# The sign of the converted weights carried through ScalarE's exponent (Prelu) instead of a VectorE operation, with the order list written anew

## The chip, the cores and the metric

The kernel runs on one core of one Trainium2 chip. The metric is the device time of one execution in microseconds (us); lower is better.

## The reference

Eight batches of attention between 512 tokens and 32 state rows in each of eight heads, both ways, give 8 x 544 rows of 512 numbers. A feed-forward layer with a rational activation follows. The weights `w_in` and `w_out`, and the coefficients, come as float64 in the kernel's inputs; the kernel turns the weights into float32 itself.

```python
scores = scale * x @ state.T ; a = softmax(scores) ; xread = a @ state      # per batch, head
scores2 = scale * state @ x.T ; a2 = softmax(scores2) ; sread = a2 @ x
rows = concat([xread, sread])                                               # 8 * 544 rows of 512
h = rows @ w_in                                                             # 512 -> 2048
P = a[0] + a[1]*h + a[2]*h**2 + a[3]*h**3
Q = 1 + abs(b[0])*abs(h) + abs(b[1])*h**2
out = (P / (Q + 1e-6)) @ w_out                                              # 2048 -> 512
```

## The kernel before

**The work.** The product of the state with `w_in` is made first for each batch and each slice of the 2048 columns ("extra", `X`, L612: 32 calls of 32 matrix products), stored in DRAM (`XS`) and read back later (`lm`). A step n (72 of them: eight column slices for each of eight batches, then eight for the state rows) then does: `F` (front, L693, twelve TensorE products of 128x512 into the PSUM tile `h`), on ScalarE `FC` (L705), `FB` (L712), `qa` (L732), `ln` (L798) and `ex` (L808), on VectorE `mu`, `po`, `qd`, `g1`, `g2`, `g3` (L716, L720, L726, L737, L743, L749), on GpSimd `gl` (L756), and on TensorE `mh` and `ml` (L766), which multiply the results `gh` and `gl` with `w_out`: four products for each of four row tiles from `gh`, two from `gl`. So `gh` (`g1`, L737) is what lets TensorE go on with a step.

**The weights.** Each float64 arrives as two 32-bit words in a tile `raw` (`lr`, DMA, 16 of 512 KB for each weight). There are 16 groups of two raw tiles: eight for `w_in`, eight for `w_out`. Per group, ScalarE runs `cp` twice (L300): it reads the upper word as a float32 and scales it by 2^-112, so that the exponent field loses its bias and the value can be shifted; the sign stays in the top bit. VectorE runs `jr` twice (L309, the low three mantissa bits out of the lower word), then `jl` (L320: the upper word shifted left by three, or-ed with these bits) and `js` (L331: the sign bit of the upper word or-ed in; its output is the tile `win_sb` for `w_in` and `cv_r` for `w_out`). After that, `X` reads `win_sb`, and `sp` (L342, L343) splits `cv_r` for `w_out` into two float32r tiles.

**What sets the order.** Each engine works through its own instructions in the order of a list of words in `ORDER` (L23), written out by hand or by a planner: a word such as `jl:3` calls the function in the table `ops` (L824) with these numbers, and so puts its instructions at the end of its engine's queue. Nothing else orders the work; an instruction then waits only for what it reads and for the buffer that it writes. All DMAs go through SyncE's queue in the list's order. The group conversions are spread over the first part of the list, between the first steps; all 16 groups are done before `g1` of step 8.

**The table of functions.** ScalarE's tables of functions are loaded once, at the start (L226), with a set that has Exp and Ln in it.

Of the kernel before, what the change touches and what calls it, by code (L numbers as in the profile page):

```python
# [13 lines left out]
AF = mybir.ActivationFunctionType  # L14
# [178 lines left out]
def attention_rational_ffn(  # L193
# [7 lines left out]
    nc = tc.nc  # L201
# [737 lines left out]
```

## Time and profile before

| | |
|---|---|
| median of 3 runs | 705.17 us (704.26 to 705.89) |
| the profiled execution | 705.25 us, of which 703.5 us are the span from the first to the last instruction |
| TensorE (PE) | 669.0 us busy (95%) |
| VectorE (DVE) | 655.5 us busy (93%) |
| ScalarE (ACT) | 523.5 us busy (74%) |
| GpSimd (POOL) | 300.4 us busy (43%) |
| mean granted TensorE clock | 0.978 of full speed |

The span is what the trace shows; 1.75 us of the execution's time lie around it. Busy time is the union of an engine's instructions. For TensorE it counts a product from its start to its modelled end, and neighbouring products overlap, so it is read best in stretches: whether the engine had a gap there, and what ended the gap. The span has two parts that are read apart: one in which the weights are converted beside the first steps (up to about 149 us), and the rest.

### The profile page before, as it was taken

How to read it: one execution, taken by the hardware profiler on the slowest of the kernel's cores; microseconds unless marked ns; L12 is line 12 of the kernel's file. 1: busy time of each engine (PE TensorE's matmuls, PEld its weight loads, DVE VectorE, ACT ScalarE, POOL GpSimd, SP SyncE). 2: the span in 40 equal slices, each digit the busy share in tenths (PEclk: the TensorE clock that was granted, in tenths of full speed). 3: DMA queues.
4: the chain of work that ended last, by engine and by line, in shares of the span. 5: the costliest groups of instructions: out<-in, count | busy, mean ns of one | idle time of the engine just before them, and what ended most of it. 6: DMA issues, size and time to landing. Idle time of an engine off the chain costs nothing.

```text
span 703.5 us, 11586 instructions
## 1 busy us (share of the span) xinstructions
PE 669.0 (95%) x4602; PEld 527.4 (75%) x4602; DVE 655.5 (93%) x605; ACT 523.5 (74%) x641; POOL 300.4 (43%) x172
## 2 busy tenths in 40 slices
PE   5788898999999999999999999999999899999997
PEld 3545565677778788878877878787878788888896
DVE  5898998999999999999999999999899989989996
ACT  4888797787766778787668687867777668667673
POOL 0033233563455445534454354435444443555542
PEclk8879999999999999999999999999999999999999
DMA  7989777513221331331311402210414001400311
GB/s 278 348 289 367 254 276 260 187 65 105 76 66 69 105 121 46 136 105 60 120 31 49 146 22 100 75 55 20 150 48 163 5 25 62 133 1 1 121 61 30
DMA packets 29434, 81.49 MB, mean 116 GB/s; under 512 B 3268, under 2 KB 3396, under 8 KB 29380
## 3 DMA queue, kind: packets, MB, share of 16 engines
q1 hardware_dynamic: 29380, 80.75, 33.2%
q8 instruction: 36, 0.59, 0.3%
q14 instruction: 18, 0.15, 0.1%
HBM read 52.95 MB, written 27.79 MB: 115 GB/s over the span
## 4 chain that ended last, share of the span: by engine, by line
PE 59%; DVE 22%; issue 4%; ACT 4%; POOL 1%; DMA 1%; SPq 0%; POOLq 0%; DVEq 0%; ACTq 0%
PE h L693 18%; DVE gh L737 4%; DVE A L743 3%; DVE A L726 3%; DVE C L716 3%; DVE C L749 3%; DVE C L720 3%; PE o__6016 L766 2%; PE o__2487 L766 2%; PE o__2431 L766 2%; PE o__5464 L766 2%; PE o__5498 L766 2%; PE o__6001 L766 2%; PE o__5476 L766 2%; PE o__2436 L766 2%
## 5 line engine op out<-in xcount | busy, mean ns | idle before, releaser
L756 POOL TENSOR_TENSOR gl<-C,L 128x1024 fp32r<-128x1024 f32 (+1 forms) x71 | 172.7, 2433 | 302.5 <-DVE C L749 223.6
L693 PE MATMUL h<-aT,m 128*128 128x512 f32 x768 | 190.0, 392 | 3.8 <-ACT xo L624 2.5
L693 PEld LDWEIGHTS h<-aT,m 128*128 128x128 f32 x768 | 142.7, 188 | 36.9 <-ACT xo L624 4.2
L705 ACT ACTIVATE C<-h,cst 128x1024 f32<-128x1024 f32 (+1 forms) x72 | 83.2, 1155 | 42.7 <-PE h L693 34.5
L712 ACT ACTIVATE A<-h,cst 128x1024 f32<-128x1024 f32 (+1 forms) x72 | 76.5, 1066 | 45.1 <-PE h L693 39.4
L743 DVE SCALAR_TENSOR_TENSOR A<-A,gh 128x1024 f32<-128x1024 f32 (+1 forms) x72 | 94.8, 1317 | 1.7
L732 ACT ACTIVATE A<-A 128x1024 f32<-128x1024 f32 (+1 forms) x72 | 72.7, 1011 | 30.2 <-DVE A L726 30.1
L737 DVE SCALAR_TENSOR_TENSOR gh<-C,cst,L 128x1024 fp32r<-128x1024 f32 (+1 forms) x72 | 91.8, 1275 | 3.5 <-ACT L L808 1.0
L749 DVE SCALAR_TENSOR_TENSOR C<-C,cst,A 128x1024 f32<-128x1024 f32 (+1 forms) x72 | 91.3, 1269 | 2.0
L726 DVE SCALAR_TENSOR_TENSOR A<-A,b0a,h 128x1024 f32<-128x1024 f32 (+1 forms) x72 | 87.0, 1211 | 6.3 <-ACT A L712 4.4
L716 DVE TENSOR_TENSOR C<-C,h 128x1024 f32<-128x1024 f32 (+1 forms) x72 | 83.1, 1155 | 8.1 <-ACT C L705 7.3
L720 DVE SCALAR_TENSOR_TENSOR C<-C,cst,h 128x1024 f32<-128x1024 f32 (+1 forms) x72 | 87.8, 1220 | 2.1
L653 POOL TENSOR_TENSOR m<-m_sb,m 128x512 fp32r<-128x512 f32 x56 | 76.7, 1379 | 28.6 <-ACT m L652 19.9
L798 ACT ACTIVATE L<-A 128x1024 f32<-128x1024 f32 (+1 forms) x72 | 73.0, 1014 | 3.2 <-POOL gl L756 0.3
L808 ACT ACTIVATE L<-L 128x1024 f32<-128x1024 f32 (+1 forms) x72 | 73.0, 1014 | 1.5
L612 PE MATMUL ps_x<-win_sb,st 64*32 64x256 f32 x1024 | 39.6, 437 | 9.9 <-DVE C L720 3.7
L343 POOL TENSOR_TENSOR wo<-cv_r,wo 128x512 fp32r<-128x512 f32 x16 | 21.9, 1382 | 56.5 <-ACT wo L342 56.3
L612 PEld LDWEIGHTS ps_x<-win_sb,st 64*32 64x32 f32 x1024 | 18.6, 119 | 26.6 <-issue 14.2
L624 ACT COPY xo<-ps_x 128x1024 f32<-128x1024 f32 (+1 forms) x32 | 29.0, 912 | 8.7 <-PE ps_x L612 4.6
L652 ACT CAST m<-m_sb 128x512 fp32r<-128x512 f32 x56 | 33.8, 613 | 0.0
L300 ACT ACTIVATE cv_y<-raw 128x512 f32<-128x512 f32 x32 | 21.4, 682 | 6.5 <-DMA raw<-in_w_in_dram 5.3
L693 PEld LDWEIGHTS h<-sh,m 128*128 128x128 f32 x192 | 24.1, 191 | 0.6
(267 smaller groups left out, 1163.9 us busy)
## 6 DMA issues: line engine op xcount, KB each, us to landing
m_sb<-m_dram SPq DMA_DIRECT2D x56, 256.0 KB, 3.3
m_dram<-xo SPq DMA_DIRECT2D x24, 512.0 KB, 3.4
out_dram<-o_sb SPq DMA_DIRECT2D x34, 256.0 KB, 4.3
raw<-in_w_in_dram SPq DMA_DIRECT2D x16, 512.0 KB, 6.1
xT_sb<-in_xT_dram SPq DMA_DIRECT2D x16, 512.0 KB, 5.1
raw<-in_w_out_dram SPq DMA_DIRECT2D x16, 512.0 KB, 6.0
x_sb<-in_x_dram SPq DMA_DIRECT2D x16, 512.0 KB, 5.2
w_in_dram<-win_sb SPq DMA_DIRECT2D x8, 512.0 KB, 5.0
```

The lines of the kernel that those rows point to most:

```text
L653: nc.gpsimd.tensor_tensor(m[:, 1], t, m[:, 0].bitcast(F32), op=ALU.subtract)
L693: nc.tensor.matmul(h[:, ci * W : (ci + 1) * W], l, r, start=(q == 0), stop=(q == len(seq) - 1),)
L705: nc.scalar.activation(e["C"], e["h"], AF.Identity, scale=cst[:, 3:4], bias=cst[:, 2:3])
L712: nc.scalar.activation(e["A"], e["h"], AF.Abs, scale=cst[:, 5:6])
L716: nc.vector.tensor_tensor(e["C"], e["C"], e["h"], op=ALU.mult)
L720: nc.vector.scalar_tensor_tensor(e["C"], e["C"], cst[:, 1:2], e["h"], op0=ALU.add, op1=ALU.mult)
L726: nc.vector.scalar_tensor_tensor(e["A"], e["A"], b0a, e["h"], op0=ALU.add, op1=ALU.mult)
L737: nc.vector.scalar_tensor_tensor(e["gh"], e["C"], cst[:, 0:1], e["L"], op0=ALU.add, op1=ALU.mult)
L743: nc.vector.scalar_tensor_tensor(e["A"], e["A"], 1.0 + 1e-6, e["gh"].bitcast(F32), op0=ALU.add, op1=ALU.mult)
L749: nc.vector.scalar_tensor_tensor(e["C"], e["C"], cst[:, 0:1], e["A"], op0=ALU.add, op1=ALU.subtract)
L756: eng.tensor_tensor(e["gl"], e["C"], e["L"], op=ALU.mult)
L766: nc.tensor.matmul(O[t], e[l][:, j * W + t * P : j * W + (t + 1) * P], wo[:, k, 2 * u + j, :], start=(place == FIRST[n // U, t] and i + j ...
```

## The change

`cp` uses the function Prelu with alpha = 2^32 in place of Copy. A positive value is only scaled by 2^-112, as before. A negative one is multiplied by 2^32 as well, which adds 32 to its exponent field; since that field is small after the scaling, this sets a bit of it that is free otherwise. The shift by three in `jl` moves that bit into the place of the sign. So `js` has nothing left to do: it goes, 16 calls in all, and `jl` writes `win_sb` itself for `w_in`. `ORDER` is a new list: it has the same calls apart from the 16 `js`, in another order throughout.

```diff
@@ conv_parts
         nc.scalar.activation(
             CV[k][0][:, j].bitcast(F32),
             RAW[i][:, :, 1].bitcast(F32),
-            AF.Copy,
+            AF.Prelu,
             scale=2.0**-112,
+            alpha=2.0**32,
         )
@@ join_low
     def join_low(k):
-        y, r = CV[k]
-        nc.vector.scalar_tensor_tensor(
-            r, y, 3, r, op0=ALU.logical_shift_left, op1=ALU.bitwise_or
-        )
-
-    def join_sign(k):
         what, u = groups[k]
         y, r = [t.rearrange("p j f -> p (j f)") for t in CV[k]]
         w = r
         if what == "in":
             win_t[u] = ld.tile([P, NP, CW], F32, name="win_sb", tag="win", bufs=3)
             w = win_t[u].rearrange("p c f -> p (c f)").bitcast(I32)
         nc.vector.scalar_tensor_tensor(
-            w, y, -(2**31), r, op0=ALU.bitwise_and, op1=ALU.bitwise_or
+            w, y, 3, r, op0=ALU.logical_shift_left, op1=ALU.bitwise_or
         )
@@ ops
         "jl": join_low,
-        "js": join_sign,
@@ ORDER
...
```

Line numbers of the changed kernel are a few lower: `cp` is L299, `jl` L325, `X` L606, `F` L687, `mh` and `ml` L760, `po` L714, `mu` L710, `qd` L720, `g1` L731, `fo` L635.

**VectorE, where the third and fourth group are joined, just ahead of the first steps' `qd`.** Before:

```order
L320 SCALAR_TENSOR_TENSOR cv_r<-cv_y,cv_r 128x1024
L331 SCALAR_TENSOR_TENSOR win_sb<-cv_y,cv_r 128x1024
L641 TENSOR_TENSOR m<-ps_x,m 128x512
L309 TENSOR_SCALAR cv_r<-raw 128x512 x2
L320 SCALAR_TENSOR_TENSOR cv_r<-cv_y,cv_r 128x1024
L331 SCALAR_TENSOR_TENSOR cv_r<-cv_y,cv_r 128x1024
L726 SCALAR_TENSOR_TENSOR A<-A,b0a,h 128x1024
```

Now:

```order
L635 TENSOR_TENSOR m<-ps_x,m 128x512
L309 TENSOR_SCALAR cv_r<-raw 128x512 x2
L325 SCALAR_TENSOR_TENSOR win_sb<-cv_y,cv_r 128x1024
L309 TENSOR_SCALAR cv_r<-raw 128x512 x2
L720 SCALAR_TENSOR_TENSOR A<-A,b0a,h 128x1024
L325 SCALAR_TENSOR_TENSOR cv_r<-cv_y,cv_r 128x1024
```

Two operations per group are one now, and the first `qd` stands ahead of the fourth group's join.

**ScalarE, from the start of its queue** (`cv_y` is what `cp` writes; the rows with `e` are Exp). Before:

```order
L226 ACT_TABLE_LOAD
L300 ACTIVATE cv_y<-raw 128x512 x2
L251 COPY cst<-ps_c__122 128x6
L420 COPY sT<-ps_sc__126 128x512
L420 COPY sT<-ps_sc__125 128x512
L300 ACTIVATE cv_y<-raw 128x512
L453 ACTIVATE e_190,r_191<-sT,cm 128x512
L300 ACTIVATE cv_y<-raw 128x512
L496 ACTIVATE e_170<-e_170 128x512
```

Now:

```order
L225 ACT_TABLE_LOAD
L299 ACTIVATE cv_y<-raw 128x512 x2
L250 COPY cst<-ps_c__131 128x6
L414 COPY sT<-ps_sc__112 128x512
L414 COPY sT<-ps_sc__113 128x512
L299 ACTIVATE cv_y<-raw 128x512
L631 CAST m<-ps_x 128x512
L618 COPY xo<-ps_x 128x512
L447 ACTIVATE e_178,r_179<-sT,cm 128x512 x2
```

The conversions keep their places among the Exp calls, and the load at the start is the only table load among the 590 rows of either queue.

**TensorE, after the front products of step 15** (`h` rows are `F`, `gh` and `gl` rows are `mh` and `ml`). The last row is, in both, the first product that reads step 15's `gh`. Before, step 15's `F` ends 70 products ahead of it, five rows above this piece:

```order
L766 MATMUL o__1800<-wo,gl 128x512 x2
L766 MATMUL o__1823<-wo,gl 128x512 x4
L693 MATMUL h<-aT,m 128x512 x6
L766 MATMUL o__1828<-wo,gl 128x512 x2
L766 MATMUL o__1828<-wo,gh 128x512 x4
L693 MATMUL h<-aT,m 128x512 x6
L766 MATMUL o__1828<-wo,gl 128x512 x2
L766 MATMUL o__1800<-wo,gh 128x512 x4
L693 MATMUL h<-aT,m 128x512 x6
L766 MATMUL o__1837<-wo,gh 128x512 x4
L693 MATMUL h<-aT,m 128x512 x6
L766 MATMUL o__1837<-wo,gh 128x512 x4
```

Now it ends 54 products ahead, two rows above this piece:

```order
L760 MATMUL o__1804<-wo,gl 128x512 x4
L687 MATMUL h<-aT,m 128x512 x12
L760 MATMUL o__1819<-wo,gl 128x512 x2
L760 MATMUL o__1852<-wo,gl 128x512 x2
L760 MATMUL o__1814<-wo,gl 128x512 x2
L760 MATMUL o__1804<-wo,gl 128x512 x2
L760 MATMUL o__1814<-wo,gh 128x512 x4
L760 MATMUL o__1852<-wo,gh 128x512 x4
L687 MATMUL h<-aT,m 128x512 x12
L760 MATMUL o__1814<-wo,gh 128x512 x4
L760 MATMUL o__1819<-wo,gl 128x512 x2
L760 MATMUL o__1814<-wo,gh 128x512 x4
```

So 16 products fewer stand between step 15's `F` and the first reader of its `gh`.

## Rows read from the trace of the kernel before

**Rows 1.** The busy time of the engines in four stretches of the span: the start up to the first `g1` (43.54 us), the same from VectorE's first uninterrupted work on (11.01 us), from there to the eighth `g1` (148.75 us), and the rest up to TensorE's last product. Columns: the stretch, its length; busy us (number of instructions) of PE, PE's weight loads, DVE, ACT, POOL; granted TensorE clock as a share of full speed, DMA share, GB/s.

```profile
0.00:43.54 43.54, 30.16 (x409) 18.96 (x413) 33.84 (x49) 30.17 (x47) 3.23 (x8) 0.78 0.81 305
11.01:43.54 32.53, 24.28 (x359) 15.02 (x363) 30.36 (x44) 26.75 (x42) 2.53 (x2) 0.76 0.80 299
43.54:148.75 105.21, 94.34 (x1154) 62.43 (x1147) 97.38 (x102) 86.55 (x115) 40.28 (x24) 0.96 0.74 262
148.75:699.00 550.25, 544.45 (x3052) 446.04 (x3050) 524.27 (x457) 406.21 (x479) 256.90 (x140) 1.00 0.22 73
```

**Rows 2.** Groups of instructions: line, engine, operation, output and inputs, shapes, number | busy us, mean ns of one | idle time of the engine before them, and what ended it. First the conversion's own lines, then other ScalarE operations of the same shape or of the table.

```profile
L331 DVE SCALAR_TENSOR_TENSOR win_sb<-cv_y,cv_r 128x1024 int32<-128x1024 int32 x8 | 10.8, 1345 | 0.3
L331 DVE SCALAR_TENSOR_TENSOR cv_r<-cv_y,cv_r 128x1024 int32<-128x1024 int32 x8 | 9.8, 1221 | 0.2
L320 DVE SCALAR_TENSOR_TENSOR cv_r<-cv_y,cv_r 128x1024 int32<-128x1024 int32 x16 | 20.5, 1280 | 2.6 <-ACT cv_y L300 2.0
L300 ACT ACTIVATE cv_y<-raw 128x512 f32<-128x512 f32 x32 | 21.4, 682 | 6.5 <-DMA raw<-in_w_in_dram 5.3 <-DMA raw<-in_w_out_dram 1.3
L342 ACT CAST wo<-cv_r 128x512 fp32r<-128x512 f32 x16 | 9.6, 618 | 0.5 <-DVE cv_r L331 0.5
L453 ACT ACTIVATE e<-sT,cm 128x512 f32<-128x512 f32 x16 | 11.5, 720 | 2.8 <-DVE cm L434 2.7
L226 ACT ACT_TABLE_LOAD x1 | 1.3, 1283 | 0.7 <-PEq L919 0.7
```

**Rows 3.** VectorE's instructions in order of time: start us, duration us, line, operation, output and inputs, shapes, number [idle time before it and what ended it]. The five `js` ahead of the first `g1`, what follows the first of them, that first `g1`, the last `js`, and the eighth `g1`.

```profile
7.66 1.22 DVE L331 SCALAR_TENSOR_TENSOR win_sb<-cv_y,cv_r 128x1024 int32<-128x1024 int32 x1
11.01 0.69 DVE L424 TENSOR_REDUCE cm<-sT 128x1 f32<-128x512 f32 x1 [2.12 <-ACT sT L420]
19.57 1.23 DVE L331 SCALAR_TENSOR_TENSOR win_sb<-cv_y,cv_r 128x1024 int32<-128x1024 int32 x1
27.15 1.22 DVE L331 SCALAR_TENSOR_TENSOR win_sb<-cv_y,cv_r 128x1024 int32<-128x1024 int32 x1
31.08 1.22 DVE L331 SCALAR_TENSOR_TENSOR cv_r<-cv_y,cv_r 128x1024 int32<-128x1024 int32 x1
41.80 1.23 DVE L331 SCALAR_TENSOR_TENSOR win_sb<-cv_y,cv_r 128x1024 int32<-128x1024 int32 x1
43.54 1.28 DVE L737 SCALAR_TENSOR_TENSOR gh<-C,cst,L 128x1024 fp32r<-128x1024 f32 x1
...
140.29 1.23 DVE L331 SCALAR_TENSOR_TENSOR cv_r<-cv_y,cv_r 128x1024 int32<-128x1024 int32 x1
148.75 1.28 DVE L737 SCALAR_TENSOR_TENSOR gh<-C,cst,L 128x1024 fp32r<-128x1024 f32 x1
```

**Rows 4.** TensorE's waits between 11 and 149 us, longest first: engine, the waiting tile and line <- whom it waited for: us in total, times, longest us.

```profile
PE ps_x L612 <- DVE C L720: 3.7, 1, 3.7
PE ps_x L612 <- ACT xo L624: 3.7, 3, 2.2
PE h L693 <- ACT xo L624: 2.5, 3, 1.6
PE ps_x L612 <- DVE e L472: 2.3, 1, 2.3
PE ps_e L440 <- DVE m L641: 2.1, 1, 2.1
PE h L693 <- DVE C L720: 1.2, 1, 1.2
PE o__652 L766 <- ACT sr L557: 1.0, 1, 1.0
```

**Rows 5.** One piece of the chain of work that ended last, in the second part of the span: start us, us, engine, tile, line, number of instructions.

```profile
156.38 2.72 PE h L693 x12
```

**Rows 6.** Step 15 in order of time (columns as in rows 3), on three engines: its last front products (the first six of a run of 18), its `FB` on ScalarE, its `g1` on VectorE, and the first TensorE products that read `gh` of step 15.

```profile
212.16 4.24 PE L693 MATMUL h<-aT,m 128*128 128x512 f32 x18
```

```profile
213.72 1.12 ACT L712 ACTIVATE A<-h,cst 128x1024 f32<-128x1024 f32 x1 [2.66 <-PE h L693]
223.63 1.28 DVE L737 SCALAR_TENSOR_TENSOR gh<-C,cst,L 128x1024 fp32r<-128x1024 f32 x1
229.65 1.07 PE L766 MATMUL o__1837<-wo,gh 128*128 128x512 f32 x4
```

327 rows, old and new, of the table ORDER are left out of this document.

## The prediction

> **What bounds the kernel now.** I read the busy time by stretches first, because the page's totals mix two parts that have different limits. After the eighth `g1` TensorE has work in 544.45 of 550.25 us, at a granted clock of 1.00, and twelve of its 128x512 products take 2.72 us on the chain that ended last, 0.227 us each [rows 1, 5]. VectorE has work in 524.27 of these 550.25 us, 95%. So from 149 us on TensorE sets the pace, and what could be won there is its 5.8 us without work. Ahead of that it is another picture. Between 43.54 and 148.75 us VectorE is the engine with the largest share, 97.38 of 105.21 us (93%), with TensorE at 94.34 (90%), ScalarE at 86.55 (82%) and the DMA engines at 0.74 [rows 1]. Between 11.01 and 43.54 us VectorE works 30.36 of 32.53 us, again 93%, while TensorE has gaps and a granted clock of 0.76, a mean between its two levels, 1.2 and 2.4 GHz [rows 1]. TensorE's waits say the same: those with a releaser of their own add up to 16.5 us between 11 and 149 us, 9.3 of them for VectorE (3.7 + 2.3 + 2.1 + 1.2) and 7.2 for ScalarE [rows 4]. The reader is to see in them that the early part is held by VectorE and that TensorE is close behind. Since everything after 149 us is a queue of TensorE work, time that TensorE gains early is kept to the end.
>
> **The change, part by part.** *The 16 sign operations.* They are 10.8 + 9.8 = 20.6 us of VectorE [rows 2], and all lie between 7.66 and 141.52 us [rows 3], in the part that VectorE holds. What of it shortens the span is limited by the engine that comes next, so I take the two stretches apart.
>
> *Up to the first `g1`.* Five of the 16 lie here [rows 3], 6.1 us. Behind the first VectorE sits idle for 2.12 us until ScalarE's copy of the scores is there [rows 3], so its 1.22 us stay hidden. The other four, 4.9 us, lie in the stretch in which VectorE has only 2.2 us of gaps [rows 1]. The bounds are 0 (the raw tiles arrive no sooner: the DMA share is 0.80 here, and ScalarE and TensorE are at 82% and 75% [rows 1]) and 4.9. I take 3.5, nearer the upper end, as no other engine is within ten points of VectorE's share.
>
> *From the first to the eighth `g1`.* The other eleven lie here, 20.6 - 6.1 = 14.5 us. Without them VectorE's work in the stretch is 97.4 - 14.5 = 82.9 us, less than TensorE's 94.34 and ScalarE's 86.55 [rows 1]. So TensorE takes over. If it never waited, the stretch would be 94.3 us, 10.9 shorter; the lower bound is 0, if the waits for ScalarE and the DMAs simply take the places of those for VectorE. In the later part TensorE reaches 99% with VectorE at 95%; here it would run beside ScalarE at 86.55 of about 97 us, 89%. I take 97% for TensorE, 94.34 / 0.97 = 97.3 us, 7.9 us shorter. TensorE could also get shorter itself, as the clock of the stretch is 0.96 [rows 1]: at 1.00 that is up to 4% of 94.3, 3.8 us; I keep it for the upper end. The waits of TensorE for VectorE, 9.3 us, are a check from another side: 3.5 + 7.9 = 11.4 is of their size, a little over.
>
> *Prelu for Copy on ScalarE*, 32 calls of 0.682 us [rows 2]. The trace has no Prelu. The nearest rows of the shape 128x512 are the plain cast of L342, 0.618, and the Exp of L453 with its own bias and sum, 0.720 [rows 2]: that is 32 x -0.064 = -2.0 to 32 x 0.038 = +1.2 us of ScalarE. I take 0: it is the same instruction with the same operands except one constant. ScalarE at 82 to 89% hides either; if it were the bound, all of it would show.
>
> *`jl` into `win_sb`.* Eight of the 16 `jl` now write the tile that `js` wrote. `js` into `win_sb` took 1.345 us on average, with one of 2.19 among them, and into `cv_r` 1.221 [rows 2]; `jl` takes 1.280 now. At most 8 x 0.12 = 1.0 us on VectorE, hidden once TensorE is the bound: 0. The DMAs are the same in number and size.
>
> *The list.* It has the same calls apart from `js`, and no engine's work grows. What it can change is TensorE's waits. After 149 us there are 5.8 us to win; what can be lost is a rival below. I take 0.
>
> **The sum.** 3.5 + 7.9 = 11.4 us less, all at the side of TensorE. The profiled execution took 705.25 us (span 703.5), next to the median of 705.17, so the forecast is 705.25 - 11.4 = 693.8 us.
>
> **The rivals.** *All of it comes back.* If TensorE's clock rises with fewer gaps and the waits for ScalarE go too, the 20.6 us come off whole: 705.25 - 20.6 = 684.7. For it: the granted clock of 0.76 ahead of 43.54 us, which shows what fuller work could give back [rows 1]. Against it: TensorE, ScalarE and the DMAs would all have to be above 90% at once. 10%.
>
> *The other engines hold the early part anyway.* Each of them has 74 to 90% there [rows 1], and the 7.2 us of waits for ScalarE can grow by what those for VectorE shrink. In full this is no change, 704 to 706 us; 7%. Half of the forecast, 698 to 703, is likelier; 13%. For it: six of TensorE's waits are for an `xo` copy on ScalarE, and they add up to 6.2 us [rows 4]; against it: ScalarE is nowhere as full as VectorE.
>
> *Slower: the new list starves TensorE in the later part.* The place is the stretch between a step's `F` and its first `mh`. For step 15 the list before has 70 products in it, 70 x 0.227 = 15.9 us, and the new one 54, 12.3 us. In the trace step 15's `F` ends at about 213.6 us (six products into the run that starts at 212.16), its `gh` is done at 224.9, 11.3 us later, and is read at 229.65: 4.7 us to spare [rows 6]. With 3.6 us less cover, 1.1 us are left. The point from which it decides is a chain from `F` to `gh` that is over 1.1 us longer than this one. If each of the 56 steps from 8 to 63 lost 0.3 us so, that would be 17 us, against 11.4 won: 705.25 + 17 - 11.4 = 711. Against it: on average over these steps I count 19.6 us of cover before and 18.8 now, with the smallest the same, 12.3; and the new list queues `qd`, `qa`, `ln`, `ex` and `g1` of step 15 without another step's between them, where the old one put step 16's and 17's between. 6%.
>
> *Slower: Prelu is not in the loaded table.* Each change between Prelu and Exp or Ln would then need a load. By the list I count 27 such changes; the load at the start took 1.283 us [rows 2], so 34.6 us more of ScalarE. Its work up to the eighth `g1` would be 30.17 + 86.55 + 34.6 = 151.3 us [rows 1], above the 148.75 that the part takes; at 93%, VectorE's share now, it would be 162.7 us, and the time 705.25 + 14 = 719. Against it: the changed ScalarE queue has one table load among its 590 rows, as before. 2%. The Trainium skill, "ScalarE: Activation LUTs", in "Table sets: the hidden batching unit", speaks against mixing functions: functions are loaded in named sets, and for the set with Exp and Ln it names these two and leaves the rest open; it counts about 2.7 us for every switch. By that figure the 27 changes would be an estimated 72 us of ScalarE and the time some 40 us longer again. No run here shows yet which functions the set holds.
>
> **How the numbers follow.** The likeliest case, TensorE taking over from VectorE in the early part, has 62%: 693.8, by its bounds 689 to 698. With the whole gain 10%, half of it 13%, none 7%, slower 6 + 2%. The range of 8 in 10 goes from 686 (a part of the whole gain) to 702 (most of the half gain): it leaves out the 7% of no change, the 8% of slower and about 5% more at its ends. A measurement of this kernel tells some 0.2%, 1.4 us, from no change. Faster by more than that, below 703.8: 62 + 10 + 13 = 85%. Within it: 7%. Slower: 8%.
>
> **What would show it.** Right: one join per group on VectorE and some 20 us less work there; the eighth `g1` at about 137 us in place of 148.75; TensorE's waits for VectorE ahead of it below 3 us, its clock there above 0.96; the stretch after it still about 550 us with TensorE without gaps; `cp` at 0.65 to 0.72 us. It is wrong if the eighth `g1` comes as early as forecast and the time doesn't (the list then loses it later), if `cp` takes over 0.75 us, if a second table load appears, or if the eighth `g1` stays where it is with ScalarE or a raw tile ahead of VectorE.

## The result: 689.75 us, 2.2% less, and the profile after

The changed kernel takes 689.75 us (median, 689.24 to 690.54), the kernel before beside it 705.53. The ratio is 0.978, with a 95% interval of 0.9761 to 0.9798. The forecast was 693.8 us, in a range of 686 to 702. In the profiled executions the span goes from 703.5 to 688.7 us.

The busy times by stretches, cut at the same places as [rows 1]: up to the first `g1`, from there to the eighth, and the rest up to TensorE's last product (columns as in [rows 1]).

```profile
0.00:43.81 43.81, 30.56 (x450) 19.06 (x450) 28.43 (x47) 30.29 (x48) 3.22 (x8) 0.84 0.83 306
43.81:140.94 97.13, 89.86 (x1099) 60.51 (x1100) 84.64 (x88) 85.16 (x115) 42.41 (x24) 0.98 0.80 283
140.94:684.30 543.36, 541.47 (x3054) 445.73 (x3052) 507.02 (x457) 408.07 (x480) 253.07 (x140) 1.00 0.22 74
```

Each stretch less the same one of before:

| stretch | forecast | measured |
|---|---|---|
| up to the first `g1` | -3.5 | 43.81 - 43.54 = +0.3 |
| first to eighth `g1` | -7.9 | 97.13 - 105.21 = -8.1 |
| eighth `g1` to TensorE's last product | 0 | 543.36 - 550.25 = -6.9 |
| together | -11.4 | -14.7 |

So one term is right in size, one came to nothing, and the largest gap is in a stretch in which I expected no change. In that last stretch VectorE runs as many instructions as before, 457, in 507.02 us in place of 524.27.

The conversion's groups, for [rows 2], columns as there:

```profile
L299 ACT ACTIVATE cv_y<-raw 128x512 f32<-128x512 f32 x32 | 21.9, 695 | 11.1 <-DMA raw<-in_w_in_dram 8.7 <-DMA raw<-in_w_out_dram 2.4
L325 DVE SCALAR_TENSOR_TENSOR win_sb<-cv_y,cv_r 128x1024 int32<-128x1024 int32 x8 | 10.9, 1358 | 0.5 <-ACT cst L250 0.3
L325 DVE SCALAR_TENSOR_TENSOR cv_r<-cv_y,cv_r 128x1024 int32<-128x1024 int32 x8 | 9.7, 1215 | 0.4
```

One join per group is left, as long as before. The Prelu takes 0.695 us in place of 0.682, and now waits 11.1 us for raw tiles where it waited 6.5.

TensorE's longest waits between 11 and 141 us, for [rows 4]:

```profile
PE ps_x L606 <- ACT xo L618: 6.1, 4, 2.7
PE ps_x L606 <- DVE C L714: 4.6, 1, 4.6
PE ps_x L606 <- DVE r L479: 1.0, 1, 1.0
```

The longest pieces of the chain of waits between 43 and 141 us (start us, us, what):

```profile
46.72 7.47 DMA raw<-in_w_in_dram
...
70.00 6.02 DMA m_dram<-xo
...
79.90 3.96 DMA m_dram<-xo
...
87.13 7.10 DMA raw<-in_w_in_dram
...
103.11 4.91 DMA m_dram<-xo
```

`xo` is the copy of the extra product on ScalarE (L618), and `m_dram<-xo` its store. The reader is to see that up to 109 us the chain now runs through raw loads, stores and the `xo` copies between them: they are 39 of its 65 us there. From 109 to 141 us TensorE's products are 26 of 32. VectorE has 5 us of the whole.

TensorE's waits behind 149 us, first of the kernel before, then of the changed one:

```profile
PE o__4881 L766 <- POOL gl L756: 1.8, 1, 1.8
PE ps_sr L566 <- ACT sr L557: 1.5, 1, 1.5
PE o__3121 L766 <- POOL gl L756: 0.9, 1, 0.9
PE ps_e L440 <- ACT L L808: 0.8, 1, 0.8
```

```profile
PE o__4923 L760 <- POOL gl L750: 1.0, 1, 1.0
PE o__2418 L760 <- POOL gl L750: 0.5, 1, 0.5
PE o__1819 L760 <- POOL gl L750: 0.4, 1, 0.4
```

### The profile page after: what moved, and what is told of

Same layout as the page of the kernel before. It is cut to its first block, busy times and chain, and to the rows that moved or that the text cites. A ratio compares the mean times of both kernels' runs of the same rounds, so it can differ in the third digit from the quotient of the medians.

```text
span 688.7 us, 11564 instructions
## 1 busy us (share of the span) xinstructions
PE 661.9 (96%) x4602; PEld 525.3 (76%) x4602; DVE 620.1 (90%) x589; ACT 524.1 (76%) x641; POOL 298.7 (43%) x172
## 4 chain that ended last, share of the span: by engine, by line
PE 77%; DVE 7%; DMA 6%; ACT 5%; issue 2%; POOL 1%; SPq 0%; POOLq 0%; ACTq 0%; DVEq 0%
PE h L687 25%; DMA m_dram<-xo 3%; DMA raw<-in_w_in_dram 2%; ACT xo L618 2%; PE o__3063 L760 2%; PE ps_x L606 2%; PE o__5992 L760 2%; PE o__3659 L760 2%; PE o__4266 L760 2%; PE o__3652 L760 2%; PE o__3604 L760 2%; PE o__5977 L760 2%; PE o__5430 L760 2%; PE o__3107 L760 2%; PE o__4244 L760 2%
## 5 line engine op out<-in xcount | busy, mean ns | idle before, releaser
L750 POOL TENSOR_TENSOR gl<-C,L 128x1024 fp32r<-128x1024 f32 (+1 forms) x71 | 168.9, 2379 | 271.1 <-DVE C L743 170.0
L687 PE MATMUL h<-aT,m 128*128 128x512 f32 x768 | 188.6, 392 | 0.8 <-ACT xo L618 0.8
L687 PEld LDWEIGHTS h<-aT,m 128*128 128x128 f32 x768 | 143.1, 188 | 33.1 <-ACT xo L618 2.9
L731 DVE SCALAR_TENSOR_TENSOR gh<-C,cst,L 128x1024 fp32r<-128x1024 f32 (+1 forms) x72 | 95.6, 1328 | 13.1 <-ACT L L802 9.5
L720 DVE SCALAR_TENSOR_TENSOR A<-A,b0a,h 128x1024 f32<-128x1024 f32 (+1 forms) x72 | 87.4, 1214 | 14.2 <-ACT A L706 10.4
L647 POOL TENSOR_TENSOR m<-m_sb,m 128x512 fp32r<-128x512 f32 x56 | 75.0, 1348 | 46.1 <-ACT m L646 22.0
L743 DVE SCALAR_TENSOR_TENSOR C<-C,cst,A 128x1024 f32<-128x1024 f32 (+1 forms) x72 | 91.0, 1263 | 2.1
L714 DVE SCALAR_TENSOR_TENSOR C<-C,cst,h 128x1024 f32<-128x1024 f32 (+1 forms) x72 | 87.7, 1219 | 1.9
L737 DVE SCALAR_TENSOR_TENSOR A<-A,gh 128x1024 f32<-128x1024 f32 (+1 forms) x72 | 87.5, 1216 | 1.7
L710 DVE TENSOR_TENSOR C<-C,h 128x1024 f32<-128x1024 f32 (+1 forms) x72 | 83.0, 1154 | 5.3 <-ACT C L699 2.7
L606 PE MATMUL ps_x<-win_sb,st 64*32 64x256 f32 x1024 | 39.6, 432 | 12.3 <-ACT xo L618 6.1
L337 POOL TENSOR_TENSOR wo<-cv_r,wo 128x512 fp32r<-128x512 f32 x16 | 23.3, 1476 | 59.8 <-ACT wo L336 59.6
L606 PEld LDWEIGHTS ps_x<-win_sb,st 64*32 64x32 f32 x1024 | 18.5, 116 | 28.1 <-issue 10.8
L618 ACT COPY xo<-ps_x 128x1024 f32<-128x1024 f32 (+1 forms) x32 | 28.8, 908 | 5.3 <-DMA m_dram<-xo 4.1
L299 ACT ACTIVATE cv_y<-raw 128x512 f32<-128x512 f32 x32 | 21.9, 695 | 11.1 <-DMA raw<-in_w_in_dram 8.7
L687 PEld LDWEIGHTS h<-sh,m 128*128 128x128 f32 x192 | 24.1, 191 | 0.6
```

What stands on the lines that cost most here:

```text
L647: nc.gpsimd.tensor_tensor(m[:, 1], t, m[:, 0].bitcast(F32), op=ALU.subtract)
L687: nc.tensor.matmul(h[:, ci * W : (ci + 1) * W], l, r, start=(q == 0), stop=(q == len(seq) - 1),)
L710: nc.vector.tensor_tensor(e["C"], e["C"], e["h"], op=ALU.mult)
L714: nc.vector.scalar_tensor_tensor(e["C"], e["C"], cst[:, 1:2], e["h"], op0=ALU.add, op1=ALU.mult)
L720: nc.vector.scalar_tensor_tensor(e["A"], e["A"], b0a, e["h"], op0=ALU.add, op1=ALU.mult)
L731: nc.vector.scalar_tensor_tensor(e["gh"], e["C"], cst[:, 0:1], e["L"], op0=ALU.add, op1=ALU.mult)
```

## The experiments

The change has two parts that can be had apart: the removal of the 16 `js` (with Prelu), and the new list. The list again has an early half, with the conversions, and a later one. The place at which both halves can be joined is the ninth `g1`, when TensorE has about the same 3010 products left in either list. The table has every run that takes these apart; times are the median of the runs, and in us of the profiled execution the eighth and ninth `g1` and what follows the ninth up to TensorE's last product.

| kernel | early list | `js` | later list | median | 8th `g1` | 9th `g1` | rest |
|---|---|---|---|---|---|---|---|
| before | old | yes | old | 705.53 | 148.75 | 158.81 | 540.19 |
| Prelu alone | old | yes | old | 705.65 | 149.32 | 159.40 | 540.09 |
| old list without `js` | old | no | old | 701.25 | 143.73 | 153.60 | 539.95 |
| old, then new | old | no | new | 695.38 | 147.69 | 157.56 | 533.64 |
| new list with `js` | new | yes | new | 705.82 | 155.42 | 165.48 | 533.07 |
| new, then old | new | no | old | 698.28 | 141.22 | 151.32 | 540.55 |
| after | new | no | new | 689.75 | 140.94 | 151.04 | 533.26 |

### The removal alone, in the old list

```diff
 kernel before, ORDER without its 16 words js:0 to js:15
-            AF.Copy,
+            AF.Prelu,
             scale=2.0**-112,
+            alpha=2.0**32,
...
-            w, y, -(2**31), r, op0=ALU.bitwise_and, op1=ALU.bitwise_or
+            w, y, 3, r, op0=ALU.logical_shift_left, op1=ALU.bitwise_or
```

> The change's arithmetic in the old list: Prelu in the conversions, the 16 sign operations gone, every other call in its old place. Theory, the sign operations' 20.6 us of VectorE are what the early part was held by: most of the gain comes without a new list, the eighth g1 at 137 to 142 us (148.75 before) and a time of 691 to 697 us. Rival, the new list carries the gain because the old one was laid out around the sign operations: VectorE only gets gaps where they stood, the eighth g1 at 146 us or later, and 701 to 705 us.

Measured: 701.25 us (699.77 to 702.63), ratio 0.9935 (0.9912 to 0.9959). The removal alone gives 4 us: the theory fell. The rival held in the time, but not in the eighth `g1`, which is at 143.73 us where it had 146 or later. VectorE's longest waits between 11 and 144 us show where room went:

```profile
DVE cv_r L311 <- DMA raw<-in_w_in_dram: 4.0, 2, 2.4
DVE cm L420 <- ACT sT L416: 3.7, 1, 3.7
DVE A L722 <- ACT C L701: 3.3, 2, 2.0
DVE m L637 <- ACT m L633: 2.7, 3, 1.1
```

In the kernel before, the longest of these was 2.1 us, and all with a name came to 9.9 us; here they come to 22.8. VectorE was freed and then waited in its old order for raw tiles and ScalarE. These waits alone don't tell the two lists apart, as they come to 18.2 us in the changed kernel. The chain of waits does: between the first and the eighth `g1` VectorE still has some 31 of its 100 us here, and 5 of 97 in the changed kernel.

### The list alone, with the sign operations put back

```diff
 changed kernel, a word js:k behind each jl:k
-            AF.Prelu,
+            AF.Copy,
             scale=2.0**-112,
-            alpha=2.0**32,
...
+        nc.vector.scalar_tensor_tensor(
+            r, y, 3, r, op0=ALU.logical_shift_left, op1=ALU.bitwise_or
+        )
+    def join_sign(k):
...
-            w, y, 3, r, op0=ALU.logical_shift_left, op1=ALU.bitwise_or
+            w, y, -(2**31), r, op0=ALU.bitwise_and, op1=ALU.bitwise_or
```

> The other half: the new list, with Copy and with each sign operation put back right behind its join. Theory (the sign operations hold the early part): the gain goes, 700 to 706 us, with the first g1 at about 48 us and the eighth at 150 to 155. Rival (the list carries the gain): 690 to 696 us. If list and removal each carry a part, both this one and the old list without sign operations lie between.

Measured: 705.82 us, ratio 1.0007 (0.9984 to 1.003); the first `g1` at 47.02 us, the eighth at 155.42. TensorE's longest waits between 11 and 156 us:

```profile
PE ps_x L614 <- DVE C L722: 9.5, 3, 5.8
PE ps_x L614 <- DVE A L728: 3.6, 1, 3.6
PE ps_x L614 <- DVE win_sb L333: 2.3, 2, 1.4
...
PE ps_x L614 <- DVE m L643: 2.0, 3, 1.2
```

The waits for VectorE are 17.4 us here and 4.6 + 1.0 = 5.6 in the rows shown of the changed kernel. On the chain between the first and the eighth `g1` VectorE has some 62 of 108 us here. The new early list needs the room on VectorE: with `js` it is 6.7 us later at the eighth `g1` than the old list, without `js` 7.8 us earlier. The time comes out even, since the new later list gives 7 us back.

### Prelu alone

```diff
 kernel before
-            AF.Copy,
+            AF.Prelu,
             scale=2.0**-112,
+            alpha=1.0,
```

> The kernel before with Prelu and alpha = 1 in the 32 conversions, the sign operations kept: Prelu's own price. Theory, Prelu costs what Copy costs: 705 us, within 1.4, the 32 conversions at 0.67 to 0.70 us each and one table load. Rival, it costs more: at 0.75 us or above ScalarE gets 2 us or more of work beside VectorE, and the time rises by up to that; with further table loads of 1.28 us each by 14 us and more.

Measured: 705.65 us, ratio 0.9991 (0.9967 to 1.0015). The group of the 32 calls:

```profile
L300 ACT ACTIVATE cv_y<-raw 128x512 f32<-128x512 f32 x32 | 21.4, 681 | 7.1 <-DMA raw<-in_w_in_dram 5.1 <-DMA raw<-in_w_out_dram 2.0
```

Prelu costs what Copy did, 0.681 against 0.682 us.

### VectorE's work put back, with nobody waiting for it

```diff
 changed kernel, a word jd:k behind each jl:k
+    def join_dummy(k):
+        y, r = [t.rearrange("p j f -> p (j f)") for t in CV[k]]
+        nc.vector.scalar_tensor_tensor(
+            y, y, 3, r, op0=ALU.logical_shift_left, op1=ALU.bitwise_or
+        )
...
+        "jd": join_dummy,
```

> The changed kernel with one VectorE operation of the sign operation's form and size put behind each of the 16 joins; it writes a tile that nobody reads any more, so no later step waits for its result. It tells VectorE's time from the length of a group's path. Theory, VectorE's time in the early part is what counts: 702 to 707 us, like the new list with the real sign operations (705.8). Rival, the path from the raw tile to the extra products got shorter by one step and that is the gain: at most 693 us.

Measured: 705.9 us, ratio 1.0001 (0.9986 to 1.0016); the first `g1` at 47.01, the eighth at 157.27, 16.3 later. The group that was put back:

```profile
L334 DVE SCALAR_TENSOR_TENSOR cv_y<-cv_y,cv_r 128x1024 int32<-128x1024 int32 x16 | 24.4, 1527 | 0.6
```

So in the new list VectorE's time counts, two thirds of it (16.3 of 24.4 us), and not the length of the path from the raw tile to the weights. The dummy also holds its `cv_y` a little longer, but among ScalarE's waits of this run there is none for VectorE at `cv_y`.

### Half of each `xo` store

```diff
 changed kernel
-        nc.sync.dma_start(m32[e, u, :, q0:], XO.pop(i)[:, q0:])
+        nc.sync.dma_start(m32[e, u, :, 1:], XO.pop(i)[:, 1:])
...
-        nc.sync.dma_start(t, m32[n // U // 2, n % U, :, n // U % 2])
+        nc.sync.dma_start(t, m32[n // U // 2, n % U, :, 1])
```

> The changed kernel, with the 24 stores of 512 KB of the extra products cut to 256 KB; every later read takes the half that was stored, so half of the values read back are not those of the reference. Theory from the trace of the changed kernel, where stores of xo and loads of raw tiles make up 30% of the chain between the first and the eighth g1 (97 us): the early part is now held by the DMAs, and with 6 MB less to store the eighth g1 comes at 131 to 136 us in place of 140.9, and the time is 680 to 686 us. Rival, as forecast, TensorE holds it: its work is unchanged, so the eighth g1 stays at 139 to 142 us and the time at 688 to 691.

Measured: 685.34 us, ratio 0.971 (0.9656 to 0.9763). From its first `g1` to its eighth, columns as in [rows 1]:

```profile
43.58:135.58 92.00, 87.98 (x1098) 60.07 (x1099) 84.45 (x87) 84.13 (x113) 42.80 (x24) 1.00 0.72 250
```

The stretch is 5.1 us shorter than in the changed kernel, with nearly the same work on VectorE and ScalarE, and the rest as long (533.23 us behind the ninth `g1`). The medians, 689.75 and 685.34, say the same, and their runs don't overlap. So the stores do hold the early part once VectorE has room.

### The same cut in the old list without `js`

```diff
 old list without js, the two lines above edited in the same way
```

> The old list with Prelu and without js, and the xo stores cut to 256 KB for the batch pairs that store 512 KB (the later reads take the stored half, so the values of half of the steps are not those of the reference). Theory (stores and raw loads hold the early part in either list once the sign operations are gone): the eighth g1 comes about 5 us sooner than without the cut, from 143.7 to 148 (two runs of this early list) to 138 to 143, and the time is 695 to 697.5. Rival (the old list is held by its own order, VectorE waiting for ScalarE's copies and conversions): under 1.5 us, 700 to 702.

Measured: 700.51 us, ratio 0.9929 (0.9907 to 0.995), next to 0.9935 with whole stores; the eighth `g1` at 143.53 against 143.73. The rival held: in the old list the stores don't matter. That its own order holds it is the reading that is left; no run shows which words. Behind the ninth `g1` this profile has 538.70 us, 1.25 less than with whole stores, and it lacks the low clock that the last section describes.

### The two halves of the list joined the other way

```diff
 ORDER = the new list up to the ninth g1, then the old list's remaining words ("new, then old");
 and the old list without js up to the ninth g1, then the new list's remaining words ("old, then new")
```

> The changed kernel with a list put together: the new list up to the ninth g1 (step 8), then what is left in the old list's order. Theory, the 3.9 us less of TensorE gaps after the eighth g1 (5.8 before, 1.9 after) come from the order there: 692 to 696 us against 689.75 for the whole new list. Rival, they come from the state that a shorter early part leaves: 688 to 691.

> The reverse: the old list without its sign operations up to the ninth g1, then what is left in the new list's order. Theory (the later order brings its 3.9 us by itself): 695 to 698.5 us against 701.25 for the whole old list without sign operations. Rival (the early part's state): 700 to 702.5.

Measured: "new, then old" 698.28 us (ratio 0.989, 0.987 to 0.9911), later than the 692 to 696 that I expected; "old, then new" 695.38 (0.9841, 0.9816 to 0.9866), as expected. In the table the rest behind the ninth `g1` is 540.0 to 540.6 us with the old later words and 533.1 to 533.6 with the new ones, whatever stands ahead (538.70 in the old list with half the stores, above). So the later half of the list is worth some 7 us, which is nearly half of the gain; by the medians it is 5.9 behind the old early half and 8.5 behind the new one. What the table also shows: two kernels with the same early words, "old list without `js`" and "old, then new", differ by 4 us at the eighth `g1`. Single readings of the early part are no better than that.

### Why the later half of the old list is slower

Two kernels, both from the kernel before. In the first, one word is moved, at the 1.8 us wait for `gl`:

```diff
-g2:52 col_exp:7:0 fd:47:2 FC:53 row_eps:7 FB:53 qd:53 qa:53 g3:52 ...
+g2:52 g3:52 col_exp:7:0 fd:47:2 FC:53 row_eps:7 FB:53 qd:53 qa:53 ...
```

> The kernel before with one word of its list moved: VectorE's g3 of step 52 stands directly behind its g2, ahead of row_eps and qd:53. In the trace of before, these take 0.17 + 0.35 + 1.18 = 1.7 us between the two, GpSimd's gl waits for g3, and TensorE waits 1.83 us for gl; in the 5 us behind that gap the granted clock is 0.66 (5 x 0.34 = 1.7 us lost). Theory (the later list wins by taking such waits away, and the clock falls because of the gap): gap and dip both go, 3.5 us, about 701.9 us, and the granted clock is 1.00 in every stretch of 5 us there. Rival: the gap goes and the dip stays, as it has another cause: 703.6. Second rival: the later qd:53 brings a new wait of the same size: 705.4.

Measured: 706.39 us, ratio 1.0016 (0.9993 to 1.0039): no change, as in the second rival. TensorE's products around the place, in order of time, before and then with the word moved (start us, us, line, output and inputs [idle time and what ended it]):

```profile
559.18 0.73 PE L766 MATMUL o__4881<-wo,gl 128*128 128x512 f32 x2 [1.83 <-POOL gl L756]
...
564.56 1.09 PE L766 MATMUL o__4891<-wo,gh 128*128 128x512 f32 x4
565.49 1.03 PE L440 MATMUL ps_a<-ident,e 128*128 128x128 f32 x8
```

```profile
557.71 0.72 PE L770 MATMUL o__4881<-wo,gl 128*128 128x512 f32 x2 [0.41 <-POOL gl L760]
...
561.46 1.09 PE L770 MATMUL o__4891<-wo,gh 128*128 128x512 f32 x4
564.52 1.09 PE L444 MATMUL ps_a<-ident,e 128*128 128x128 f32 x8 [1.97 <-DVE r L485]
```

The wait for `gl` fell from 1.83 to 0.41 us, and the way from there to `o__4891` from 5.38 to 3.75. The latter is the clock: the stretch of before that follows the gap has a granted clock of 0.66 (last but two of the columns, as in [rows 1]), and 1.00 with the word moved.

```profile
560.00:565.00 5.00, 5.00 (x20) 4.17 (x19) 4.90 (x7) 3.47 (x4) 3.18 (x3) 0.66 0.17 52
```

So TensorE has `o__4891` 3.1 us earlier, and then waits 1.97 for VectorE's `r`; the remaining 1.0 us is gone by the end (540.38 us behind the ninth `g1`, 540.19 before). One wait taken away brought another: with `g3` ahead of it, `qd:53` starts 1.27 us later, and what hangs on it too. What made `g3` late stayed as it was. In the kernel before, `g2` of step 52 takes 3.39 us, held up by GpSimd's `gl` (last section):

```profile
550.42 3.39 DVE L743 SCALAR_TENSOR_TENSOR A<-A,gh 128x1024 f32<-128x1024 f32 x1
```

```profile
550.33 2.40 POOL L756 TENSOR_TENSOR gl<-C,L 128x1024 fp32r<-128x1024 f32 x1 [7.22 <-PE o__4881 L766]
```

With the word moved it takes 3.38. Whether VectorE as a whole is late there is what the second kernel tests:

```diff
 ORDER without mu:16 to mu:63
```

> The kernel before without mu of steps 16 to 63 (48 VectorE operations of 1.21 us, so P of these steps lacks a factor h and their part of the output is not the reference's); list and everything else as before. VectorE has 514.6 us of work in the 540.2 from the ninth g1 to TensorE's end, and some 58 us less now. Theory (in the old list TensorE's later gaps come from VectorE being late, 95% full): the stretch from the ninth g1 comes to 532 to 535 us, as in the new list, and the time to 697 to 700. Rival (they come from where the words of TensorE, ScalarE and GpSimd stand, whatever room VectorE has): 538.5 to 540, 703.5 to 705.5; the waits for gl and for ScalarE's sr stay as they are.

Measured: 699.92 us, ratio 0.9915 (0.9885 to 0.9945). From the ninth `g1` to TensorE's last product:

```profile
159.47:694.12 534.65, 530.73 (x3008) 437.36 (x3006) 464.44 (x401) 398.12 (x472) 255.25 (x138) 1.00 0.22 75
```

534.65 us in place of 540.19: with 50.1 us less work on VectorE the old list gets 5.5 of the 7 us that the new one gets. The theory held in its numbers. But TensorE's time without work is the smaller part of it, 5.80 us before and 3.92 now; its busy time fell from 534.39 to 530.73, of which 1.7 is the low clock, which this profile doesn't have, and 2.0 is not traced. The wait for ScalarE's `sr` stays (1.4 us), as the rival said of it, and so does one of 1.3 for `gl`. A second rival is left: `mu` lies on the path from `F` to `g1`, so this run also shortens each step's path by 1.21 us, and does not tell that from the room on VectorE.

### The stores from another engine's queue

```diff
 changed kernel
-        nc.sync.dma_start(m32[e, u, :, q0:], XO.pop(i)[:, q0:])
+        nc.scalar.dma_start(m32[e, u, :, q0:], XO.pop(i)[:, q0:])
```

> The changed kernel with the 32 stores of the extra products issued from ScalarE's queue in place of SyncE's; sizes and data are the same. In the changed kernel's trace ScalarE waits for such stores (6.0, 4.9 and 4.0 us each on the chain) beside raw loads of 7 us. Theory, the DMAs' bytes hold the early part: no gain, 688 to 692 us, slower by what ScalarE spends on issuing. Rival, a store waits its turn behind raw loads of the same queue: with a queue of its own the eighth g1 comes at 136 to 139 us and the time is 684 to 688.

and with `nc.gpsimd` in place of `nc.scalar`:

> The changed kernel with the xo stores issued from GpSimd's queue in place of SyncE's. Theory (what holds the early part is that a store waits for its xo copy in the one queue, and the raw loads behind it wait as well): the raw loads no longer stand behind the stores, the eighth g1 comes 2 to 5 us sooner, the time is 685 to 688. Rival (the transfers themselves hold it, and a store now stands behind gl on GpSimd, which is busy 42 of 97 us there): 690 to 700. With ScalarE's queue it was 711.

Measured: 711.44 us from ScalarE (ratio 1.0071, 1.0045 to 1.0097) and 724.93 from GpSimd (1.028, 1.0255 to 1.0304). All theories missed, the rivals too: both are far slower than expected. ScalarE's wait for the store that frees its `xo` tile, up to 160 us, from ScalarE's queue and then from GpSimd's:

```profile
ACT xo L618 <- DMA m_dram<-xo: 20.7, 11, 3.2
```

```profile
ACT xo L618 <- DMA m_dram<-xo: 30.7, 14, 8.7
```

In the changed kernel this wait is 4.1 us. A piece of GpSimd's instructions in order of time shows one way in which it comes about:

```profile
71.16 3.23 POOL L750 TENSOR_TENSOR gl<-C,L 128x1024 fp32r<-128x1024 f32 x1 [6.73 <-DVE C L743]
74.32 1.13 POOL L623 DMA_DIRECT2D m_dram<-xo  x2
```

GpSimd waits 6.73 us for `g3` and works 3.23 on `gl`; the two stores stand behind it and start one after the other. The transfer of 512 KB itself is hardly slower (4.7 us from issue to landing, 4.6 from SyncE's queue; 5.2 from ScalarE's). So a store's cost here is, at least in part, when its turn comes; how much of the 22 and 35 us that is, no run shows. The Trainium skill, "DMA: Bandwidth & Descriptors", in "Issuing engines are not separate DMA queues", says that transfers of all queues share the same 16 DMA engines and that another queue saves only the time to start them. The runs agree that no bandwidth is won: in the first 160 us the DMAs move 265 GB/s in the changed kernel, and 255 and 243 in these two. What they add is that the work ahead in a busy engine's queue has a price.

## Why the prediction was right, and where it was not

**VectorE holds the early part.** Right for the new list: 16 idle operations put back cost 16.2 us of the median. In the old list the same removal gives 4 us, so the profile of before did not show the whole condition: the room is of use only to an order that fills it.

**Up to the first `g1`, -3.5.** Wrong in sum, +0.3: the lower bound. But the removal did its part in the new list: its first `g1` is at 47.02 us with `js`, at 47.01 with the idle operations, and at 43.81 without either, 3.2 sooner. What used that up is the new list, which with `js` is 3.5 us later there than the old one (43.54). In the old list the removal moved nothing (43.47), so VectorE's share of [rows 1] was no proof that it led there. These are single readings; four kernels that have the old early words and `js` lie between 43.54 and 45.58. In the changed kernel the chain goes through `xo` copies and a store: `16.61 5.74 DMA m_dram<-xo` holds the next copy of `xo`, and the first `F` stands behind that. TensorE has 450 products done by then, 41 more than before, at a granted clock of 0.84 in place of 0.78.

**First to eighth `g1`, -7.9.** The size is right (-8.1), the reason only in part. It is again the sum of two: with `js` the new list needs 108.40 us here, 3.2 more than the old one, and without them 97.13, so the removal is worth 11.3, a little over my upper bound of 10.9. I had TensorE take over at 97% of the stretch. It has 92.5% (89.86 of 97.13), and the number came out because its own work fell too, by 4.5 us: 55 fewer of its products lie in the stretch (41 more lie ahead of it), and the granted clock is 0.98. What leads now up to 109 us are raw loads, `xo` copies and their stores, and halving the stores gave 5.1 us; only behind that does TensorE lead, as I had it for the whole stretch. My check was also off: waits for VectorE of at least 5.6 us are left, where I said below 3. And my 16.5 us of waits were those of the seven rows shown; the whole view of before has 19.7, of which 9.9 are for VectorE and 9.0 for ScalarE.

**Prelu, 0.** Right, by the run that has it alone. The rival of a table load per change is out: there is one load at the start. The Trainium skill's page "ScalarE: Activation LUTs", which I had cited against the change, leaves open which other functions stand in the set of Exp and Ln; the runs show that Prelu needs no load beside them.

**`jl` into `win_sb`, 0.** Right within its 1.0 us: 1.358 on average where `js` had 1.345.

**The list, 0.** This is the step that failed. The list alone does come to 0, but as two parts of some 7 us that cancel: 6.7 later at the eighth `g1`, 7.1 less behind the ninth. The first comes only with `js` in it, so change and list don't add up, as my sum had them. Of the second I had nothing: I took TensorE's 5.8 us of gaps as all there was to win, and VectorE at 95% as cover enough. The gaps did fall to 1.9 us, and TensorE's busy time by 3.0, which I had not counted: 1.7 of it is the low clock behind the gap of 1.83 us. VectorE was probably not merely beside TensorE: without `mu` the old list's later part is 5.5 us shorter too, though that run shortens each step's path as well. In the new list VectorE has the room without losing an instruction, 497.30 us for the 449 instructions behind the ninth `g1` in place of 514.55. It is 17 us that VectorE was held up by GpSimd less (last section). That they are the cause in the new list is the likely reading, not a shown one: no run puts them back alone. That my total came as near as it did is partly luck: it has 3.6 us too much ahead of the eighth `g1` and 6.9 too little behind it.

**The rivals.** No starvation of TensorE behind step 15: its waits behind 149 us are 1.0, 0.5 and 0.4 us, none for `gh`. "All of it comes back", 684.7, is near in number (689.75) but not in cause. "The other engines hold the early part anyway" is near what the old list showed.

**What stays open:** which words of the old early list keep its VectorE waiting, and so why 20.6 us less work gave 4 there. And how much of the later half's 7 us is VectorE's room.

## What to carry to other kernels

The price of a removed operation belongs to the order it is removed from: here 4 us in the old list and 16 in the new one, and the new list without the removal won nothing, so change and order are to be tried apart and together. An engine that is 95% busy beside a full TensorE may be no cover: ask what 10% more room on it would give, by leaving out some of its work, if possible work whose result nothing waits for. And before a share of busy time is taken for a bound, follow the chain of that stretch; in the changed kernel it went through stores and raw loads, which no engine's share showed.

## What the runs showed of the hardware

**VectorE and GpSimd hold each other up.** In the kernel before, three places in order of time, the GpSimd rows from its own view:

```profile
182.00 3.42 DVE L737 SCALAR_TENSOR_TENSOR gh<-C,cst,L 128x1024 fp32r<-128x1024 f32 x1 [0.57 <-ACT A L712]
...
199.79 2.37 DVE L481 TENSOR_SCALAR r<-r 128x2 f32<-128x2 f32 x1
...
308.60 1.44 DVE L434 TENSOR_SCALAR cm<-cm 128x2 f32<-128x2 f32 x1
```

```profile
181.93 2.40 POOL L756 TENSOR_TENSOR gl<-C,L 128x1024 fp32r<-128x1024 f32 x1 [2.90 <-PE o__1837 L766]
...
198.85 3.29 POOL L756 TENSOR_TENSOR gl<-C,L 128x1024 fp32r<-128x1024 f32 x1 [4.83 <-PE o__1837 L766]
...
307.61 2.40 POOL L756 TENSOR_TENSOR gl<-C,L 128x1024 fp32r<-128x1024 f32 x1 [8.03 <-DVE C L749]
```

An operation on 128x2 numbers takes 2.37 us and ends with GpSimd's `gl` (202.16 and 202.14), another ends with the third `gl` (310.04 and 310.01). A `g1`, 1.28 us by itself, takes 3.42 and ends 1.09 us behind the first `gl` (185.42 and 184.33). So a part of VectorE's busy time is time in which it is held up. It goes the other way as well: the second `gl` began while a `g1` ran (198.59 to 199.87), and took 3.29 in place of 2.40. The groups by form show some of the operations that meet this, first before, then after; `g2` (L743, now L737) and the small ones are stretched, while `po` (L720, now L714), which reads `h` from PSUM, keeps its 1.28 us:

```profile
L743 DVE SCALAR_TENSOR_TENSOR A<-A,gh 128x1024 f32<-128x1024 f32 x64 | 87.9, 1373 | 1.5
L720 DVE SCALAR_TENSOR_TENSOR C<-C,cst,h 128x1024 f32<-128x1024 f32 x64 | 81.8, 1280 | 1.9
L506 DVE TENSOR_SCALAR rs<-rs 128x32 f32<-128x32 f32 x7 | 6.6, 942 | 0.2
L434 DVE TENSOR_SCALAR cm<-cm 128x2 f32<-128x2 f32 x7 | 5.6, 803 | 0.2
```

```profile
L737 DVE SCALAR_TENSOR_TENSOR A<-A,gh 128x1024 f32<-128x1024 f32 x64 | 82.0, 1281 | 1.4
L714 DVE SCALAR_TENSOR_TENSOR C<-C,cst,h 128x1024 f32<-128x1024 f32 x64 | 81.7, 1278 | 1.6
L500 DVE TENSOR_SCALAR rs<-rs 128x32 f32<-128x32 f32 x7 | 2.1, 303 | 0.1
L428 DVE TENSOR_SCALAR cm<-cm 128x2 f32<-128x2 f32 x7 | 2.1, 300 | 0.1
```

Not every operation gains: `g1` goes from 1.341 to 1.394 us on average. Counted behind the ninth `g1`, 30 of VectorE's operations in the kernel before take over 0.3 us longer than their form usually does, 31.5 us in all, and 19 in the changed kernel, 14.7 us; each ends within 1.4 us of the end of a GpSimd operation. So the new list has fewer such meetings, and nearly all of the 17 us are theirs. TensorE's longest late wait of before comes from one of them (`g2` at 550.42, above). The Trainium skill, "SBUF — State Buffer", in "SBUF: two separate sides", states the rule: the two engines share a pair of ports under an exclusive lock, for the whole instruction, when VectorE reads two tensors from SBUF, against a GpSimd operation that reads SBUF too, or runs in a two-port mode; whichever starts first has them, and the other fully blocks. The three places agree with it, in both directions; whether the operations on 128x2 numbers run in a two-port mode, no view here shows.

**The clock behind a short gap.** The gap of 1.83 us ahead of `o__4881` (or the tile in its place) stands in five profiles with the old later words. In four of them the granted clock is lower behind it. Its mean over stretches of 5 us, where 1.00 is the level of 2.4 GHz and 0.50 that of 1.2, is 0.66 in one stretch in two of the profiles, 0.94 and 0.72 in two stretches in the third, and 0.79 and 0.87 in the fourth, each time worth some 1.7 us (5 x 0.34). In the fifth, the old list with half the stores, none follows, and none follows the gap of 1.97 us in the kernel with the word moved. Of twelve profiles none has another stretch of 5 us with a mean below 0.99 between 150 us and TensorE's last products, though waits of 1.3 to 1.5 us stand there. A gap of this length can cost its own size again, and need not.
